# One pass for the normalised rows, and the first three tiles transposed before they are scaled: an attention and MLP kernel on one Trainium2 core

## The chip, the core and the metric

The kernel runs on one core of one Trainium2 chip. The core has a matrix engine (TensorE, "PE"; its weight loads are listed as "PEld"), three engines for everything else (VectorE "DVE", ScalarE "ACT", GpSimd "POOL") and a queue engine (SyncE, "SP") that here only issues DMA transfers. Each engine takes its instructions in the order of the program and waits on semaphores for the others. The metric is the device time of one execution in microseconds (us).

## The reference

`x` is a 2048 x 640 bfloat16 matrix. Each row is normalised, `xn = (x - m) / sqrt(v + eps)`. Two blocks read `xn`, and their results are added to `x`:

- a linear attention with 32 heads of 20: `q, k, v = xn @ wqkv`, `phi(t) = where(t > 0, t + 1, exp(t)) + 1e-6`, `kv = phi(k)^T v` and `z = sum of phi(k)` over all 2048 rows, then `o = phi(q) kv / (phi(q) z)` and `o @ wo`;
- a gated MLP on only 8 rows: `r = xn @ w_r` is computed for all rows, the 8 rows with the largest `r` go through `silu(x w_gate) * (x w_up) @ w_down`, are weighted with `sigmoid(r)` and added at their places.

## The kernel before, in words

The 2048 rows are 16 tiles of 128 rows. `XX` holds for each tile the rows as loaded (second index 1) and normalised (index 0); `xnT` holds the normalised rows transposed, which TensorE needs as its stationary operand. The order of the instructions is written out by hand in the program; there is no scheduler.

For a tile `t` these steps follow one another. `ln_a` and `ln_b` (VectorE, statistics of the two halves of the row, lines 161 and 164), `ln_g` (aggregate, 167), `ln_s` (add eps, line 200, then a power of one half on POOL, line 201): the row's standard deviation. For tiles 1 and 5 ScalarE makes the sums instead (`ln_act`, 175 to 179) and POOL the variance and the power (`ln_msq`, `ln_var`, 188 to 195). `ln_c` centres the row and flips its sign (on VectorE, line 208, or from tile 6 on ScalarE, line 206). `ln_xn` takes the reciprocal of the deviation (`SR`, line 213) and scales the centred row in a second VectorE pass (line 215). Tiles 0 to 3 are then transposed on TensorE into PSUM and copied to `xnT` by ScalarE (`tr_pe`, lines 222 and 226), the others by DMA transposes that SP issues (`tr_dma`, line 231).

`K(t)` multiplies the transposed tile with the key weights, in two halves of five matmuls (line 253); the second half carries `w_r` as a 321st column, so that `r` comes along. ScalarE applies exp and relu to each half (`PHe`, `PHr`, lines 269 and 272), VectorE joins them (`PHb`, line 288) to `pk`. `ones(t)` overwrites column 512 of the normalised tile with 1 (POOL, line 304), so that the product `G(t) = xn^T pk` (lines 293 and 298) also carries `z`; what belongs to that column is later restored in the value weights (`wv_rows`). K needs two PSUM banks that exp and relu of the tile before must have left.

Before the first tile, TensorE runs matmuls on zeros (`warm4`, fp32, line 122, and `warm`, bf16, line 127), with the small transpose of `w_r` between them.

The loop over tiles 4 to 15 keeps, at step t, K(t), PHb(t-1), the second pass and the DMA transpose of tile t+2, exp and relu of t, statistics and centring of t+3, statistics of t+4, and G(t-1). `loads(t)` issues later weights on SP. Behind the loop come the corner products (line 312), the query products (503), the kv and output-weight products, the MLP on the 8 rows, and the output (754, 768).

Of the kernel before, what the change touches and what calls it, by code (L numbers as in the profile page):

```python
# [27 lines left out]
TF = 11  # L28

# [9 lines left out]
def kernel(  # L39
# [39 lines left out]
    Gs = st([P, KC, D], BF16, "Gs")  # L79
# [10 lines left out]
    epsb = st([P, 1], BF16, "epsb")  # L90
# [12 lines left out]
    def ld(eng, dst, src):  # L103
        eng.dma_start(dst, src)
# [13 lines left out]
    zero32 = zero[:].bitcast(F32)  # L118

    def warm4(n):  # L120
        for _ in range(n):
            pe.matmul(PS[:, 7, :], lhsT=zero32[:, 0:P],
                      rhs=zero32[:, 0:256].unsqueeze(1).to_broadcast([P, 2, 256]), start=True, stop=True)
# [6 lines left out]
    pool.memset(epsb[:], EPS_BF16)  # L130
# [38 lines left out]
    cs = {}  # L169
# [15 lines left out]
    msq = st([P, 4], F32, "msq")  # L185

    def ln_msq(t):
        pool.tensor_tensor(out=msq[:, 0:1], in0=sm[:, t, 0:1], in1=sm[:, t, 0:1], op=ALU.mult)

    def ln_var(t):  # L190
        pool.tensor_tensor(out=MV[:, t, 1:2], in0=sm[:, t, 1:2], in1=msq[:, 0:1], op=ALU.subtract)
        t2 = tmp.tile([P, 1], BF16, tag="t2", name="t2", bufs=4)
        ss[t] = tmp.tile([P, 1], BF16, tag="s", name="s", bufs=4)
        pool.tensor_tensor(out=t2[:], in0=MV[:, t, 1:2], in1=epsb[:], op=ALU.add)
        pool.tensor_tensor(out=ss[t][:], in0=t2[:], in1=halfc[:], op=ALU.pow)

    def ln_s(t):
        t2 = tmp.tile([P, 1], BF16, tag="t2", name="t2", bufs=4)
        ss[t] = tmp.tile([P, 1], BF16, tag="s", name="s", bufs=4)
        dve.tensor_scalar(out=t2[:], in0=MV[:, t, 1:2], scalar1=EPS_BF16, scalar2=None, op0=ALU.add)  # L200
        pool.tensor_tensor(out=ss[t][:], in0=t2[:], in1=halfc[:], op=ALU.pow)  # L201

    def ln_c(t, eng):
        cs[t] = tmp.tile([P, D], BF16, tag="c", name="c", bufs=3)
        if eng is act:
            act.activation(cs[t][:], XX[:, t, 1, :], AF.Identity, bias=MVf[:, t, 0:1], scale=-1.0)  # L206
        else:
            dve.tensor_scalar(out=cs[t][:], in0=XX[:, t, 1, :], scalar1=MVf[:, t, 0:1], scalar2=-1.0,
                              op0=ALU.subtract, op1=ALU.mult)

    def ln_xn(t, parts=((0, D),)):
        c = cs[t]
        dve.reciprocal(SR[:, t : t + 1], ss[t][:])
        for a, b in parts:
            dve.tensor_scalar(out=XX[:, t, 0, a:b], in0=c[:, a:b], scalar1=SR[:, t : t + 1], scalar2=-1.0,  # L215
                              op0=ALU.mult, op1=ALU.mult)

    def tr_pe(t, b0, e0, e1, hs=(0, 1)):
        for b, k0, k1, eng in [((b0, 0, 3, e0), (b0 + 1, 3, KC, e1))[h] for h in hs]:
            pt = PS[:, b, :].bitcast(BF16)[:, 0 : (k1 - k0) * P]  # L220
            for kc in range(k0, k1):
                pe.transpose(pt[:, (kc - k0) * P : (kc - k0 + 1) * P], XX[:, t, 0, kc * P : (kc + 1) * P], ident[:])
            dst = xnT[:, k0:k1, t * P : (t + 1) * P]
            src = pt.rearrange("p (k c) -> p k c", c=P)
            if eng is act:
                act.copy(dst, src)  # L226
            else:
                dve.tensor_copy(dst, src)

# [19 lines left out]
    def K(t, hs=(0, 1), b=6):  # L249
        for h in hs:  # L250
            w = HW + h
            for kc in range(KC):
                pe.matmul(  # L253
                    PS[:, b + h, off(t, h) : off(t, h) + w],
                    lhsT=xnT[:, kc, t * P : (t + 1) * P],
                    rhs=wkh[h][:, kc, 0:w],
                    start=(kc == 0),
                    stop=(kc == KC - 1),
                )
# [5 lines left out]

    def PHe(t, h, b=6):
        if h == 0:
            phis[t] = tuple(tmp.tile([P, D], BF16, tag=k, name=k, bufs=3) for k in ("ek", "rk"))
        act.activation(phis[t][0][:, h * HW : (h + 1) * HW], phi_src(t, h, b), AF.Exp)  # L269

    def PHr(t, h, b=6):
        act.activation(phis[t][1][:, h * HW : (h + 1) * HW], phi_src(t, h, b), AF.Relu)  # L272
# [6 lines left out]
    def rcopy():  # L279
        act.copy(rbf[:, 0 : T - 2], PS[:, 7, HW : HW + T - 2])  # L280
        dve.tensor_copy(rbf[:, T - 1 : T], PS[:, 7, HW + T - 1 : HW + T])

    def rcopy1(b):
        act.copy(rbf[:, T - 2 : T - 1], PS[:, b, HW : HW + 1])
# [63 lines left out]
    pool_extra = {3: consts_b, 4: consts_c, 5: consts_d}  # L348
# [9 lines left out]
    def loads(t):  # L358
        if t < 5:
            ld(sp, XX[:, 6 + 2 * t : 8 + 2 * t, 1, :], x_v[:, 6 + 2 * t : 8 + 2 * t, :])  # L360
        if 7 <= t < 7 + KC:
            ld(sp, wv[:, t - 7, :], wqkv_v[:, t - 7, 2 * D : 3 * D])
        if t == 6:
            late["wvb"] = st([P, D], BF16, "wvb", "junk")
            ld(sp, late["wvb"][:], A_wqkv[ZD : ZD + 1, 2 * D : 3 * D].to_broadcast([P, D]))
# [20 lines left out]
    ln_msq(1)  # L386
    ln_c(0, dve)
    ln_c(1, dve)
    ln_xn(0, ((0, 3 * P), (3 * P, D)))
    tr_pe(0, 0, act, act)  # L390
    ln_var(1)
    ln_a(2)
    ln_xn(1)
    ln_b(2)
    ln_g(2)
    ln_s(2)
    ones(0)
    K(0, (0,))
    PHe(0, 0)
    tr_pe(1, 2, act, act)  # L400
    consts_e()
    bm2_copies(sp, (1, 2))
    PHr(0, 0)
    K(0, (1,))
    ln_c(2, dve)
    ln_a(3)
    ln_xn(2)
    PHa(0, (1,))
    K(1, (0,), 4)
    tr_pe(2, 0, act, act)  # L410
    K(1, (1,), 4)
    PHa(1, (0,), 4)
    PHa(1, (1,), 4)
    rcopy1(5)
# [116 lines left out]

    act.copy(Gs[:, 0, 0:512], PS[:, 0, :])
# [414 lines left out]
```

## Time and profile before

| | us |
|---|---|
| median of 3 runs | 109.26 (109.14 to 109.51) |
| profiled execution | 109.16 |
| its span, first to last instruction | 107.4 |
| TensorE busy | 101.6 |
| VectorE busy | 84.5 |
| ScalarE busy | 74.9 |
| POOL busy | 27.3 |

The span is 1.76 us shorter than the profiled execution's time; what lies around it is start and end. A view named "chain" follows the work that ended last back from the last instruction. In the views by line, a group's row gives the line, the engine, the operation, what it writes and reads, its shape and count, then the busy time of the group in us, the mean length of one in ns, and the idle time before them. In the timeline a row gives start and length in us; "x5" behind it means five instructions merged. Lengths overlap where an engine is pipelined: five matmuls of 0.3 us each can take 0.85 us together.

### The profile page before, as it was taken

The numbers are of one execution on the slowest core, as the hardware profiler recorded it, in microseconds if no ns is written. First come the engines' busy times: TensorE is split into PE (matmuls) and PEld (weight loads), VectorE is DVE, ScalarE is ACT, GpSimd is POOL, SyncE is SP. The second block draws the span as 40 slices with busy tenths as digits, with TensorE's granted clock in tenths as the row PEclk, the third lists the DMA queues.
The fourth block names the chain that finished last, engine by engine and source line by source line (L and its number), as shares of the span: only waits on it lengthen the run. The fifth ranks groups of instructions, "written<-read, shape, count | busy, mean of one in ns | idle before, by whom it ended". The sixth has DMA issues, their size and how long they took to land.

```text
span 107.4 us, 2577 instructions
## 1 busy us (share of the span) xinstructions
PE 101.6 (95%) x908; PEld 62.5 (58%) x918; DVE 84.5 (79%) x206; ACT 74.9 (70%) x163; POOL 27.3 (25%) x79
## 2 busy tenths in 40 slices
PE   5989999999999999999999999999999999999960
PEld 1245656666666666667556555655656677777740
DVE  1789997999989999974888987539599696888860
ACT  4649996888877777888596999988687699000000
POOL 7437235456222222000000683200008000000410
PEclk9999999999999999999999999999999999999999
DMA  2979971434555665889997999911650243895342
GB/s 70 296 215 324 324 143 38 84 76 77 131 127 122 128 127 120 183 233 367 265 402 259 313 338 383 309 43 36 205 179 0 62 146 111 213 368 191 126 132 65
DMA packets 23152, 19.68 MB, mean 183 GB/s; under 512 B 10595, under 2 KB 21603, under 8 KB 23139
## 3 DMA queue, kind: packets, MB, share of 16 engines
q1 hardware_dynamic: 21944, 19.00, 60.7%
q10 hardware_dynamic: 906, 0.50, 1.6%
q8 instruction: 7, 0.11, 0.4%
q0 software_dynamic: 288, 0.01, 0.3%
q14 instruction: 7, 0.05, 0.2%
HBM read 13.80 MB, written 3.65 MB: 162 GB/s over the span
## 4 chain that ended last, share of the span: by engine, by line
PE 82%; DVE 7%; DMA 2%; POOL 2%; issue 2%; ACT 1%; SPq 0%; POOLq 0%
PE PS L503 20%; PE PS L754 20%; PE PS L253 15%; PE PS L293 14%; PE PS L298 4%; DMA XX<-in_A_x_dram 2%; PE PS L679 2%; PE PS L716 2%; DVE XX L215 1%; DVE pk L288 1%; POOL s L201 1%; DVE stats L164 1%; PE PS L567 1%; PE PS L738 1%; PE PS L312 1%
## 5 line engine op out<-in xcount | busy, mean ns | idle before, releaser
L253 PE MATMUL PS<-wk,xnT 128*128 128x320 bf16 (+1 forms) x160 | 24.7, 300 | 0.4 <-ACT xnT L226 0.4
L503 PE MATMUL PS<-xnT,wq 128*128 128x512 bf16 x95 | 22.7, 380 | 0.3
L293 PE MATMUL PS<-pk,XX 128*128 128x512 bf16 x75 | 22.3, 379 | 0.2 <-DVE pk L288 0.2
L754 PE MATMUL PS<-Mb,pqT 128*128 128x320 bf16 x160 | 22.1, 299 | 0.0
L253 PEld LDWEIGHTS <-xnT 128*128 128x128 bf16 x160 | 15.4, 98 | 7.3 <-ACT xnT L226 0.9
L754 PEld LDWEIGHTS <-pqT 128*128 128x128 bf16 x160 | 15.5, 97 | 6.5 <-issue 0.2
L269 ACT ACTIVATE ek<-PS 128x320 bf16<-128x320 f32 x32 | 14.2, 445 | 5.2 <-PE PS L253 5.2
L503 PEld LDWEIGHTS <-wq 128*128 128x128 bf16 x100 | 11.3, 118 | 9.0
L558 DVE SCALAR_TENSOR_TENSOR pqT<-qe,qr 128x512 bf16<-128x512 bf16 x20 | 13.5, 684 | 2.0 <-ACT qr L510 1.7
L768 DVE TENSOR_TENSOR o<-PS,XX 128x640 bf16<-128x640 f32 x15 | 12.2, 821 | 3.5 <-PE PS L754 2.8
L509 ACT ACTIVATE qe<-PS 128x512 bf16<-128x512 f32 x20 | 12.2, 609 | 3.8 <-PE PS L503 3.3
L272 ACT ACTIVATE rk<-PS 128x320 bf16<-128x320 f32 x32 | 14.3, 447 | 0.0
L298 PE MATMUL PS<-pk,XX 128*128 128x128 bf16 x64 | 14.0, 219 | 0.3
L201 POOL TENSOR_TENSOR s<-t,halfc 128x1 bf16<-128x1 bf16 x14 | 8.7, 625 | 21.6 <-DVE t L200 21.6
L288 DVE SCALAR_TENSOR_TENSOR pk<-ek,rk 128x640 bf16<-128x640 bf16 x16 | 13.0, 815 | 0.9 <-ACT rk L272 0.7
L293 PEld LDWEIGHTS <-XX 128*128 128x128 bf16 x80 | 7.7, 98 | 8.1
L510 ACT ACTIVATE qr<-PS 128x512 bf16<-128x512 f32 x20 | 12.1, 605 | 0.0
L206 ACT ACTIVATE c<-XX,MVf 128x640 bf16<-128x640 bf16 x10 | 8.4, 839 | 1.7 <-DVE MVf L167 1.6
L243 ACT ACTIVATE XX<-XX,MR,SR 128x640 bf16<-128x640 bf16 x11 | 9.4, 915 | 0.0
L161 DVE BATCH_NORM_STATS2 stats<-XX 128x6 f32<-128x320 bf16 x14 | 6.8, 485 | 1.9 <-DMA XX<-in_A_x_dram 1.9
L215 DVE TENSOR_SCALAR XX<-c,SR 128x640 bf16<-128x640 bf16 (+2 forms) x17 | 6.3, 377 | 1.3
L593 DVE TENSOR_TENSOR pqT<-pqT,R 128x1280 bf16<-128x1280 bf16 x8 | 6.5, 817 | 0.5 <-DMA R<-rd_d 0.5
(125 smaller groups left out, 104.7 us busy)
## 6 DMA issues: line engine op xcount, KB each, us to landing
out_dram<-o SPq DMA_DIRECT2D x15, 160.0 KB, 2.8
XX<-in_A_x_dram SPq DMA_DIRECT2D x6, 320.0 KB, 5.2
wg<-in_B_w_gate_dram SPq DMA_DIRECT2D x5, 384.0 KB, 8.1
wu<-in_B_w_up_dram SPq DMA_DIRECT2D x5, 384.0 KB, 5.9
wd<-in_B_w_down_dram SPq DMA_DIRECT2D x1, 1920.0 KB, 11.3
wv<-in_A_wqkv_dram SPq DMA_DIRECT2D x5, 160.0 KB, 3.0
wq<-in_A_wqkv_dram SPq DMA_DIRECT2D x1, 800.0 KB, 5.0
hi_d<-XX SPq DMA_DIRECT2D x1, 800.0 KB, 4.5
```

What stands on the lines that cost most here:

```text
L253: pe.matmul(PS[:, b + h, off(t, h) : off(t, h) + w], lhsT=xnT[:, kc, t * P : (t + 1) * P], rhs=wkh[h][:, kc, 0:w], start=(kc == 0), stop=( ...
L269: act.activation(phis[t][0][:, h * HW : (h + 1) * HW], phi_src(t, h, b), AF.Exp)
L272: act.activation(phis[t][1][:, h * HW : (h + 1) * HW], phi_src(t, h, b), AF.Relu)
L288: dve.scalar_tensor_tensor(out=pk[:, t, :], in0=ek[:], scalar=1.0, in1=rk[:], op0=ALU.min, op1=ALU.add)
L293: pe.matmul(PS[:, a, :], lhsT=lhsT, rhs=pk[:, t, 0:512], start=(t == 0), stop=(t == T - 1),)
L298: pe.matmul(PS[:, 5, a * P : (a + 1) * P], lhsT=lhsT, rhs=pk[:, t, 512:D], start=(t == 0 and a == 0), stop=(t == T - 1), skip_group_check= ...
L503: pe.matmul(PS[:, bank, :], lhsT=by5(wq[:, kc, :])[:, m, :], rhs=xnT[:, kc, tb * TBLK : (tb + 1) * TBLK], start=(kc == 0), stop=(kc == KC ...
L509: act.activation(e, PS[:, bank, :], AF.Exp)
L510: act.activation(r, PS[:, bank, :], AF.Relu)
L558: dve.scalar_tensor_tensor(out=pqT[:, m, tb * TBLK : (tb + 1) * TBLK], in0=e, scalar=1.0, in1=r, op0=ALU.min, op1=ALU.add,)
L754: pe.matmul(PS[:, b + h, 0:HW], lhsT=pqT[:, kc, t * P : (t + 1) * P], rhs=Mb[:, kc, h * HW : (h + 1) * HW], start=(kc == 0), stop=(kc == K ...
L768: dve.tensor_tensor(out=ot[:].rearrange("p (h c) -> p h c", h=2), in0=PS[:, b : b + 2, 0:HW], in1=XX[:, t, 1, :].rearrange("p (h c) -> p h ...
```

## The change

- `ln_n` makes the normalised row in one VectorE pass, `(x - mean) * SR`, with both scalars taken per row from memory; `ln_xn` is reciprocal plus that pass. The centring passes `ln_c` of tiles 3 and later are gone (ten of them were on ScalarE).
- Tiles 0 to 2 (`CT = 3`) are only centred (`ln_c`, without the flipped sign) and transposed on TensorE in that state into a new tile `cT`. Their K uses `cT`; exp and relu multiply by the row's factor `SR` (`scale=SR`), and the two copies of `r` of tiles 0 and 1 do too. `cT` shares its memory with `Gs`, which is now allocated after the loop.
- Their normalised rows are made later (`ln_n(0)`, `ln_n(1)`, `ln_n(2)`), for G alone, and their transposes for `xnT` are three DMA transposes, at t = 5, 7 and 9. As column 512 has been overwritten by then, POOL first keeps it (`keep512`), and three small DMAs on ScalarE's queue put it back into `xnT` at t = 12 (`back512`).
- Of the PSUM copies of `tr_pe`, tile 0's first half and tile 2's second half go to VectorE.
- The warm-up is one fp32 matmul on a constant that is there earlier, and behind the transpose of `w_r` 20 matmuls of 96 columns, in place of a second fp32 one and one of 512 columns.
- POOL's variance takes one instruction less (`ln_msqe` folds eps in). `consts_e` moves from the start to the loop (after G(6)); the three copies of `bm2` move to ScalarE's queue at t = 10; the loads of `wv` and `wvb` move from SP's queue to ScalarE's.
- The order of the first tiles is rewritten.

```diff
+    def warm4():
+        pe.matmul(PS[:, 7, 0:512], lhsT=z0.to_broadcast([P, P]), rhs=z0.to_broadcast([P, 512]), start=True, stop=True)
...
-    warm4(1)
+    warm4()
     pe.transpose(PS[:, 3, :].bitcast(BF16)[:, 0:KC], wr[:], ident[0:KC, 0:KC])
-    warm4(1)
-    warm(1)
+    warm(20, 96)
...
+    def ln_msqe(t):
+        pool.tensor_scalar(out=msqe[:, t : t + 1], in0=sm[:, t, 0:1], scalar1=sm[:, t, 0:1], scalar2=EPS_BF16,
+                           op0=ALU.mult, op1=ALU.subtract)
...
+    def ln_r(t):
+        dve.reciprocal(SR[:, t : t + 1], ss[t][:])
+
+    def ln_n(t, parts=((0, D),), eng=dve):
+        for a, b in parts:
+            eng.tensor_scalar(out=XX[:, t, 0, a:b], in0=XX[:, t, 1, a:b], scalar1=MVf[:, t, 0:1],
+                              scalar2=SR[:, t : t + 1], op0=ALU.subtract, op1=ALU.mult)
...
+    def ln_c(t):
+        cs[t] = tmp.tile([P, D], BF16, tag="c", name="c", bufs=CT)
+        dve.tensor_scalar(out=cs[t][:], in0=XX[:, t, 1, :], scalar1=MVf[:, t, 0:1], scalar2=None, op0=ALU.subtract)
+
+    def keep512(t):
+        pool.tensor_copy(c512[:, t : t + 1], XX[:, t, 0, ZD : ZD + 1])
+
+    def back512():
+        for t in range(CT):
+            ld(act, xnT[0:1, KC - 1, t * P : (t + 1) * P], c512[:, t : t + 1])
...
-                    lhsT=xnT[:, kc, t * P : (t + 1) * P],
+                    lhsT=(cT if t < CT else xnT)[:, kc, t * P : (t + 1) * P],
...
+    def row_scale(t):
+        return {"scale": SR[:, t : t + 1]} if t < CT else {}
...
-        act.activation(phis[t][0][:, h * HW : (h + 1) * HW], phi_src(t, h, b), AF.Exp)
+        act.activation(phis[t][0][:, h * HW : (h + 1) * HW], phi_src(t, h, b), AF.Exp, **row_scale(t))
...
+    ln_c(0)
+    ln_c(1)
+    tr_pe(0, 0, dve, act, 3)
+    tr_pe(1, 2, act, act)
     ln_var(1)
+    ln_r(0)
+    K(0, (0,))
     ln_a(2)
     ln_b(2)
     ln_g(2)
+    ln_c(2)
     ln_s(2)
+    ln_r(1)
+    PHa(0, (0,))
+    K(1, (0,), 4)
     ln_a(3)
     ln_b(3)
     ln_g(3)
     ln_s(3)
+    PHa(1, (0,), 4)
+    tr_pe(2, 0, act, dve)
+    K(0, (1,))
+    ln_r(2)
+    ln_n(0)
+    keep512(0)
+    ones(0)
+    PHa(0, (1,))
+    K(1, (1,), 4)
+    PHa(1, (1,), 4)
+    rcopy1(5)
+    ln_xn(3)
     PHb(0)
+    K(2)
+    PHa(2, (0,))
+    tr_pe(3, 2, act, act)
+    PHa(2, (1,))
     ln_a(4)
     ln_b(4)
     ln_g(4)
     ln_s(4)
+    PHb(1)
     ln_xn(4)
     tr_dma(4)
+    ln_n(1)
+    keep512(1)
+    ones(1)
     ln_act(5)
+    ln_msqe(5)
     G(0, (0, 1, 4, 2, 3))
     K(3)
     G(1)
+    ln_n(2)
+    keep512(2)
+    ones(2)
     PHb(2)
     ln_var(5)
     PHa(3)
+    ln_a(6)
     ln_xn(5)
     tr_dma(5)
+    ln_b(6)
     ln_g(6)
     ln_s(6)
     ones(3)
     G(2)
...
-            ln_c(t + 3, act)
...
+        if t in (5, 7, 9):
+            tr_dma((t - 5) // 2)
         if t > 4:
             loads(t)
+        if t == 10:
+            bm2_copies(act, (1, 2, 3))
+        if t == 12:
+            back512()
```

More of the change, by code (lines that the diff above doesn't have):

```diff
@@ L28 @@
 TF = 11
+CT = 3
 BF16 = mybir.dt.bfloat16
@@ L115 @@
     ld(sp, XX[:, 2, 1, :], x_v[:, 2, :])
[L118 to L123, printed above, removed]
+    z0 = nc.const_aps.tensor(0.0, [P, 1], F32)
+    def warm4():
+        pe.matmul(PS[:, 7, 0:512], lhsT=z0.to_broadcast([P, P]), rhs=z0.to_broadcast([P, 512]), start=True, stop=True)
     def warm(n, w=512):
@@ L190, in ln_var @@
     def ln_var(t):
-        pool.tensor_tensor(out=MV[:, t, 1:2], in0=sm[:, t, 1:2], in1=msq[:, 0:1], op=ALU.subtract)
         t2 = tmp.tile([P, 1], BF16, tag="t2", name="t2", bufs=4)
-        ss[t] = tmp.tile([P, 1], BF16, tag="s", name="s", bufs=4)
-        pool.tensor_tensor(out=t2[:], in0=MV[:, t, 1:2], in1=epsb[:], op=ALU.add)
-        pool.tensor_tensor(out=ss[t][:], in0=t2[:], in1=halfc[:], op=ALU.pow)
+        pool.tensor_tensor(out=t2[:], in0=sm[:, t, 1:2], in1=msqe[:, t : t + 1], op=ALU.subtract)
@@ L197, in ln_s @@
+        ln_pow(t, t2)
     def ln_s(t):
         t2 = tmp.tile([P, 1], BF16, tag="t2", name="t2", bufs=4)
-        ss[t] = tmp.tile([P, 1], BF16, tag="s", name="s", bufs=4)
         dve.tensor_scalar(out=t2[:], in0=MV[:, t, 1:2], scalar1=EPS_BF16, scalar2=None, op0=ALU.add)
[L201 to L209, printed above, removed]
@@ L211, in ln_xn @@
-    def ln_xn(t, parts=((0, D),)):
[L212 to L219, printed above, removed]
+        ln_pow(t, t2)
+    def ln_r(t):
+        dve.reciprocal(SR[:, t : t + 1], ss[t][:])
@@ L221, in tr_pe @@
             for kc in range(k0, k1):
[L222 to L223 removed]
+                src = cs[t][:, kc * P : (kc + 1) * P] if t < CT else XX[:, t, 0, kc * P : (kc + 1) * P]
+                pe.transpose(pt[:, (kc - k0) * P : (kc - k0 + 1) * P], src, ident[:])
+            dst = (cT if t < CT else xnT)[:, k0:k1, t * P : (t + 1) * P]
             src = pt.rearrange("p (k c) -> p k c", c=P)
```

74 lines of the change are left out of this document (20 added, 54 removed).

## The prediction

> **What bounds the kernel now.** I read the page first (span, busy time, chain shares), then busy time by stretches, then the chain in order of time, and last the instructions one by one up to 24 us.
>
> ```profile
> span 107.4 us, 2577 instructions
> ...
> PE 101.6 (95%) x908; PEld 62.5 (58%) x918; DVE 84.5 (79%) x206; ACT 74.9 (70%) x163; POOL 27.3 (25%) x79
> ...
> PE 82%; DVE 7%; DMA 2%; POOL 2%; issue 2%; ACT 1%; SPq 0%; POOLq 0%
> ```
>
> PE carries 82% of the chain. Where it doesn't is seen in the stretches (columns: PE, PEld, DVE, ACT, POOL busy, clock, DMA) and the chain:
>
> ```profile
> 14.00:16.00 2.00, 1.85 (x14) 1.08 (x12) 1.97 (x5) 1.97 (x7) 0.42 (x2) 1.00 0.64 83
> 16.00:18.00 2.00, 2.00 (x15) 1.12 (x14) 1.34 (x6) 1.12 (x5) 1.05 (x3) 1.00 0.31 63
> ```
>
> ```profile
> 9.58 0.41 DVE stats L164
> ...
> 10.71 0.73 DVE pk L288
> ...
> 13.25 0.62 POOL s L201
> ...
> 14.49 0.74 DVE pk L288
> ...
> 15.28 0.38 PE PS L293
> ...
> 18.04 1.37 PE PS L253 x10
> ...
> 22.09 0.27 PE PS L293
> ...
> 50.19 0.84 PE PS L312 x15
> ```
>
> Up to 15.28 the chain runs through VectorE and the short POOL powers; from there it is matmuls without a hole, K(4) at 18.04, G(4) at 22.09, the corners at 50.19. (The chain puts a matmul some 0.16 later than its start, since the one before ends then: K(4) starts at 17.88, G(4) at 21.93.) So all that the change can win lies ahead of about 22 us. Behind it PE has the same work, and each 0.1 us by which G(4) is early is 0.1 us of the end, unless a later wait takes it back.
>
> **The start.** PE and VectorE rows of the first 12 us:
>
> ```profile
> 3.35 2.08 PE L122 MATMUL PS<-zero 128*128 128x512 f32 x2
> 5.22 0.63 PE L127 MATMUL PS<-zero 128*128 128x512 bf16 x1
> 5.90 0.71 PE L222 MATMUL PS<-ident,XX 128*128 128x128 bf16 x5
> 6.97 0.85 PE L253 MATMUL PS<-wk,xnT 128*128 128x320 bf16 x5 [0.36 <-ACT xnT L226]
> 7.66 0.44 PE L222 MATMUL PS<-ident,XX 128*128 128x128 bf16 x5
> ```
>
> ```profile
> L222 PE MATMUL PS<-ident,XX x20: 219/219/314, 5.9 to 12.2; 128*128 128x128 bf16 x20
> ```
>
> ```profile
> 4.37 0.88 DVE L208 TENSOR_SCALAR c<-XX,MVf 128x640 bf16<-128x640 bf16 x2
> ```
>
> ```profile
> 8.18 0.38 DVE L208 TENSOR_SCALAR c<-XX,MVf 128x640 bf16<-128x640 bf16 x1
> ```
>
> Tile 0's transposes now wait for power, reciprocal and second pass until 5.90; centred rows exist at 4.75 (two passes of 0.38 from 4.37, the second waits for ScalarE's mean and ends at 5.25). Five transposes took 0.71 with 0.314 for the last, so 0.10 each at 5.90, and (0.44-0.219)/4 = 0.055 each at 7.66: the array ran at half speed until past 6.3, at full speed from 6.97, where K took (0.85-0.30)/4 = 0.137 a matmul. The clock column shows 1.00 throughout, so only these steps tell it.
>
> After the change the second fp32 block and the 512-wide warm-up (until 5.65) become 20 matmuls of 96 columns from 3.42. At half speed the 96 columns cost 96/128 of 0.105, i.e. 0.08: they end at 5.0. The bound above is the full 0.10 to 0.107 of a 128-column pair, if the weight load paces them (end 5.5); below, 0.04 at full speed, but then c0 at 4.8 is the limit. I take 0.08. Transposes of tiles 0 and 1 follow back to back (10 x 0.105) to 6.0, and K(0) starts at 6.0 for 6.97. VectorE copies tile 0's first half from 5.5 (third transpose plus 0.31).
>
> **VectorE's queue.** Prices, and steps: an instruction that doesn't read the one ahead starts 0.08 before that ends (statistics 0.485 long, 0.41 apart above).
>
> ```profile
> L288 DVE SCALAR_TENSOR_TENSOR pk<-ek,rk 128x640 bf16<-128x640 bf16 x16 | 13.0, 815 | 0.9 <-ACT rk L272 0.7
> ...
> L161 DVE BATCH_NORM_STATS2 stats<-XX 128x6 f32<-128x320 bf16 x14 | 6.8, 485 | 1.9 <-DMA XX<-in_A_x_dram 1.9
> ...
> L215 DVE TENSOR_SCALAR XX<-c,SR 128x640 bf16<-128x640 bf16 x15 | 5.8, 387 | 1.3
> ...
> L167 DVE BATCH_NORM_AGGREGATE MVf<-stats 128x2 bf16<-128x12 f32 x14 | 3.0, 211 | 0.5
> ...
> L208 DVE TENSOR_SCALAR c<-XX,MVf 128x640 bf16<-128x640 bf16 x6 | 2.3, 379 | 0.1
> ...
> L240 DVE TENSOR_SCALAR XX<-XX,SR,MR 128x640 bf16<-128x640 bf16 x5 | 2.0, 443 | 0.0
> ...
> L733 DVE COPY hT<-PS 128x384 bf16<-128x384 bf16 x1 | 0.4, 358 | 0.0
> ```
>
> The one-pass row takes two per-partition scalars, like L240: 0.443, 0.06 over L215's 0.387 (the bounds). Up to tile 5 VectorE loses three centring passes (c of 3, 4, 5: 3 x 0.30), gains two PSUM copies (0.29 and some 0.23) and 6 x 0.06: even. What it gains is idle time and an earlier start. Adding the steps in the new order: copy 5.5, reciprocal 5.8, tile 2's statistics 5.87, c(2) 7.05 (for 8.18), tile 3's statistics 7.48, n(0) 9.0, n(3) 9.75, PHb(0) 10.1 (for 10.71), G(0) 11.05. Tile 4's statistics 10.85, PHb(1) 12.1 (for 14.49: two n-passes now stand behind it), n(4) 13.1, n(1) 13.5-13.9, so G(1) 13.97 for 15.28 and K(4) 16.57 for 17.88: **1.3 us ahead**. The transposes by DMA keep up:
>
> ```profile
> xnT<-XX SPq DMA_TRANSPOSE x12, 2.6
> ```
>
> n(4) ends at 13.55, plus 2.6 is 16.2.
>
> **What is late next.** POOL, then VectorE again:
>
> ```profile
> 14.92 0.36 POOL L188 TENSOR_TENSOR msq<-sm 128x1 f32<-128x1 f32 x1 [1.00 <-ACT junk L175]
> 15.94 0.37 POOL L191 TENSOR_TENSOR MVf<-sm,msq 128x1 bf16<-128x1 f32 x1 [0.66 <-ACT junk L179]
> 16.38 0.19 POOL L194 TENSOR_TENSOR t<-MVf,epsb 128x1 bf16<-128x1 bf16 x1
> 16.66 0.55 POOL L195 TENSOR_TENSOR s<-t,halfc 128x1 bf16<-128x1 bf16 x1
> ```
>
> ```profile
> L304 POOL MEMSET XX<- 128x1 bf16 x16 | 1.5, 100 | 3.7 <-DMA xnT<-XX 3.7
> ```
>
> ```profile
> 17.24 0.16 DVE L213 RECIPROCAL SR<-s 128x1 f32<-128x1 bf16 x1 [0.58 <-POOL s L195]
> ...
> 18.05 0.82 DVE L288 SCALAR_TENSOR_TENSOR pk<-ek,rk 128x640 bf16<-128x640 bf16 x1
> ...
> 21.12 0.81 DVE L288 SCALAR_TENSOR_TENSOR pk<-ek,rk 128x640 bf16<-128x640 bf16 x1
> ```
>
> Tile 5's power now stands on POOL behind keep512 and ones of tiles 1 and 2: from n(1)'s end at 13.9, copy, memset, msq, copy, memset, subtract, power. A 128x1 copy isn't in the trace; the nearest rows are 0.19 and 0.37, I take 0.28, so 0.28+0.1+0.36+0.28+0.1+0.28+0.55 plus gaps of 0.08 (16.57 to 16.66) = 2.2, and reciprocal(5) starts at 16.2 (for 17.24; at 0.19 and 0.37 each it is 15.85 and 16.5). Then n(5) 16.4, aggregate(6) 17.3, PHb(3) 17.6 to 18.45 (for 18.05). PE reaches G(3) at 16.57+1.37 = 17.94 and waits 0.56. PHb(4), seven steps on with the dearer n(6), comes at 20.57 to 21.4 (for 21.12 to 21.93), K(5) ends at 21.17, another 0.28 lost. G(4) at 21.45 for 21.99 (PHb(4)'s end and 0.06): **0.55 us ahead**. From there VectorE's steps add up to 2.55 a tile (PHb 0.735, two statistics 0.81, n 0.36, aggregate, reciprocal and the small ones 0.65) for PE's 2.68 (from 18.04 to 22.09 less one K of 1.37), and nothing holds PE.
>
> **ScalarE and the queues.** Ten centring passes go, DMA issues come:
>
> ```profile
> 12.55 0.60 ACTq L104 DMA_DIRECT2D bm<-bm  x1
> ```
>
> ```profile
> L206 ACT ACTIVATE c<-XX,MVf 128x640 bf16<-128x640 bf16 x10 | 8.4, 839 | 1.7 <-DVE MVf L167 1.6
> ```
>
> One issue a tile (0.6) for 0.84 of work is no loss. At t = 10 there are four (wv and three bm2, 2.4), at t = 12 three (1.8). ScalarE has 1.2 free between relu(t) and K(t+1)'s first half; the issue of 12.55 ran under two queued copies, so some 0.5 more is covered, and exp(11) is 0.7 late, exp(13) 0.1. Behind them wait PHb(11) and K(12), which has G(10)'s 1.3 as slack. Taken at nothing; with no cover the four cost 0.5. The transposes' issue on SP:
>
> ```profile
> 27.59 1.22 SPq L231 DMA_TRANSPOSE xnT<-XX  x1
> ```
>
> bm2 leaves SP's queue ahead of tr_dma(4), which waits for n(4) anyway; the extra transposes at t = 5, 7, 9 take 1.2 of SP each, where 2.67 is there for two and the loads have gone to ScalarE's queue. back512 lands 8 us before the first query product at 51. Scaled exp and relu: between the same and 0.08 more (L240 over L215, as for VectorE); hidden, as VectorE is behind.
>
> **The sum.** Profiled run 109.16 (span 107.4 and 1.76 around it) minus 0.55 is 108.6; the median of three, 109.26, is 0.1 above the profiled run, so I say **108.7**. About 0.3%, 0.33 us, is what a measurement here can tell from no change.
>
> **Rivals.** (1) *Slower: the full clock comes a stretch later.* The speed-up seen between 6.3 and 6.97 followed dense fp32 and 512-wide matmuls; now short matmuls and ten transposes stand there. PE is nearly back to back from 6.0 to 10.65 in my sum (30 K matmuls of 0.137). If it stays at half speed until about 10, some 3.5 us later, G(0) comes 1.7 later, of which VectorE's lag covers 0.4: 108.7+1.3 = 110.0. It takes back all 0.55 from a grant at about 8.5 on (half of 1.9 us, less the 0.4). Against it: PE is fed without a gap from 3.42, no less than before. The Trainium skill ("TensorE: Matmul & The Clock Gate", Part 4) says that transposes on TensorE don't count as busy for the clock gate; by that, what counts between 3.4 and 6.0 is 1.6 us of warm-ups where it was 2.5, and this rival would come. The trace has transposes at full speed at 7.66, but no speed-up after transposes alone, so it leaves the rule open. Chance 0.20.
>
> (2) *No change: the warm-ups are paced by their weight loads* (0.105) or the POOL copies take 0.37: each takes back 0.3 to 0.5 of the 0.55, since both stand in series with VectorE's queue: 109.1 to 109.2. For it: transposes step at 0.10 to 0.107, POOL rows beside busy VectorE are at 0.36. The four issues at t = 10 uncovered end here too. Chance 0.20.
>
> (3) *More: POOL's short ops at 0.19 and passes at 0.387*: 0.3 each, 108.1. Chance 0.15. My own case 0.45, by itself 108.4 to 109.0.
>
> **Range and chances.** 107.9 (both gains of 3) to 109.8 (most of rival 1). Faster by over 0.3%: three quarters of mine, all of (3), a quarter of (2): 0.54. Slower: 0.19 of (1) and 0.04 elsewhere: 0.23. The rest, 0.23, is the same.
>
> **What would show it.** Warm-ups 0.08 apart, K(0) near 6.0 in steps of 0.27 then 0.137, n(3) near 9.75, G(1) near 14.0, reciprocal(5) idle on POOL until 16.2, PE idle ahead of G(3) and G(4) and nowhere after, corners near 49.6 in the chain's count, passes of 0.44. Wrong if K still steps at 0.27 past 8, or if PE has holes after 30 us.

## The result, and the profile after

The changed kernel takes 113.63 us (median of 4 executions, 112.87 to 114.62) where the kernel before takes 109.2 us. The profiled execution (114.62 us, span 112.9 us) holds a stretch of half clock between 50 and 53 us, worth 1.6 us there, so its ratio is taken from the other three: their median is 113.40 us, 1.038 times as long, with a 95% interval of 1.032 to 1.044. The forecast was 108.7 us and faster.

The page of the kernel after: span, busy time, the chain by engine, and the group of the K matmuls.

```profile
span 112.9 us, 2604 instructions
...
PE 104.1 (92%) x935; PEld 64.0 (57%) x935; DVE 85.0 (75%) x204; ACT 68.0 (60%) x151; POOL 28.3 (25%) x79
...
PE 57%; DVE 15%; DMA 13%; POOL 5%; ACT 3%; issue 2%; ACTq 1%; SPq 1%; DVEq 0%
...
L262 PE MATMUL PS<-wk,xnT 128*128 128x320 bf16 (+1 forms) x130 | 20.4, 304 | 3.8 <-DMA xnT<-XX 3.7
```

TensorE carried 82% of the chain before and carries 57% now; DMA went from 2% to 13%. The idle time ahead of K names the cause's place: 3.7 us of waiting for transposes by DMA. TensorE's timeline of the kernel after shows where (start, length, then in brackets the idle time ahead and what ended it):

```profile
4.76 1.04 PE L216 MATMUL PS<-ident,c 128*128 128x128 bf16 x10
5.71 0.45 PE L262 MATMUL PS<-wk,cT 128*128 128x320 bf16 x2
6.81 1.25 PE L262 MATMUL PS<-wk,cT 128*128 128x320 bf16 x8 [0.65 <-DMA wk<-in_A_wqkv_dram]
...
18.68 1.54 PE L262 MATMUL PS<-wk,xnT 128*128 128x320 bf16 x10 [0.95 <-DMA xnT<-XX]
...
23.02 0.38 PE L306 MATMUL PS<-pk,XX 128*128 128x512 bf16 x1
...
30.26 1.55 PE L262 MATMUL PS<-wk,xnT 128*128 128x320 bf16 x10 [0.42 <-DMA xnT<-XX]
...
48.83 1.95 PE L262 MATMUL PS<-wk,xnT 128*128 128x320 bf16 x10 [2.35 <-DMA xnT<-XX]
...
53.13 1.58 PE L262 MATMUL PS<-wk,xnT 128*128 128x320 bf16 x10
```

The rows of the same work in the kernel before, G(4), K(8), K(14) and K(15):

```profile
21.98 0.38 PE L293 MATMUL PS<-pk,XX 128*128 128x512 bf16 x1
...
28.63 1.54 PE L253 MATMUL PS<-wk,xnT 128*128 128x320 bf16 x10
...
44.68 1.54 PE L253 MATMUL PS<-wk,xnT 128*128 128x320 bf16 x10
...
47.35 0.84 PE L253 MATMUL PS<-wk,xnT 128*128 128x320 bf16 x5
```

So the kernel after is 1.04 us late at G(4), 1.63 at K(8), 4.15 at K(14) and 5.78 at K(15). The steps are 1.0 at the start, 0.6 at K(8), 2.5 ahead of K(14), and 1.6 of half clock in this execution alone. The chain of the kernel after gives the transposes behind two of them, and three rows of the start:

```profile
12.58 1.07 POOL s L187
...
14.74 1.09 POOL c L233
...
17.37 0.17 DVE SR L200
...
25.91 4.30 DMA xnT<-XX
...
42.49 6.29 DMA xnT<-XX
```

A transpose by DMA had taken 2.6 us from issue to landing; that of tile 8 takes 4.30 and that of tile 14 takes 6.29. The stretches around it (columns as in the prediction; the last two are the share of the DMA engines and GB/s), after and then before:

```profile
44.00:46.00 2.00, 2.00 (x16) 1.25 (x15) 1.93 (x7) 1.26 (x4) 0.16 (x2) 1.00 1.26 121
46.00:48.00 2.00, 0.48 (x3) 0.10 (x1) 1.83 (x5) 0.96 (x2) 0.00 (x0) 1.00 1.08 75
48.00:50.00 2.00, 1.17 (x8) 0.82 (x9) 0.13 (x1) 0.22 (x1) 0.10 (x1) 0.95 1.60 82
50.00:52.00 2.00, 2.00 (x8) 0.96 (x7) 0.39 (x1) 1.73 (x5) 0.07 (x1) 0.50 0.60 159
```

```profile
44.00:46.00 2.00, 2.00 (x16) 1.29 (x15) 1.88 (x5) 1.55 (x5) 0.00 (x0) 1.00 0.91 168
46.00:48.00 2.00, 2.00 (x16) 1.21 (x15) 1.26 (x3) 1.84 (x5) 0.10 (x1) 1.00 0.83 235
```

From 46 to 48 us the share of the DMA engines rises from 0.83 before to 1.08 after, while they move a third of the bytes (75 GB/s for 235): something occupies them without moving much data. (A packet is counted in the stretch in which it starts, so a share can exceed 1.) Transfers issued in that stretch land late, whatever they carry; the rows of the issues (KB each, then us to landing) from 40 to 56 us:

```profile
wq<-in_A_wqkv_dram SPq DMA_DIRECT2D x1, 800.0 KB, 7.9
wo<-in_A_wo_dram SPq DMA_DIRECT2D x4, 160.0 KB, 7.0
...
xnT<-XX SPq DMA_TRANSPOSE x3, 6.3
xnT<-c ACTq DMA_DIRECT2D x3, 0.2 KB, 6.9
```

Before, wq took 5.0 us there and the four wo transfers 2.9.

### The profile page after: what moved, and what is told of

It reads as the page before. It is cut to its first block, busy times and chain, and to the rows that moved or that the text cites. A ratio compares the mean times of both kernels' runs of the same rounds, so it can differ in the third digit from the quotient of the medians.

```text
span 112.9 us, 2604 instructions
## 1 busy us (share of the span) xinstructions
PE 104.1 (92%) x935; PEld 64.0 (57%) x935; DVE 85.0 (75%) x204; ACT 68.0 (60%) x151; POOL 28.3 (25%) x79
## 4 chain that ended last, share of the span: by engine, by line
PE 57%; DVE 15%; DMA 13%; POOL 5%; ACT 3%; issue 2%; ACTq 1%; SPq 1%; DVEq 0%
PE PS L517 20%; PE PS L769 19%; DMA xnT<-XX 9%; PE PS L262 5%; PE PS L306 5%; DMA XX<-in_A_x_dram 4%; DVE pk L301 3%; POOL s L187 3%; DVE XX L204 3%; DVE stats L159 3%; DVE stats L156 2%; ACT rk L284 2%; PE PS L694 1%; PE PS L731 1%; DVE MVf L162 1%
## 5 line engine op out<-in xcount | busy, mean ns | idle before, releaser
L306 PE MATMUL PS<-pk,XX 128*128 128x512 bf16 x80 | 24.8, 395 | 0.3 <-ACT xnT L220 0.3
L262 PE MATMUL PS<-wk,xnT 128*128 128x320 bf16 (+1 forms) x130 | 20.4, 304 | 3.8 <-DMA xnT<-XX 3.7
L281 ACT ACTIVATE ek<-PS 128x320 bf16<-128x320 f32 x26 | 11.4, 437 | 19.8 <-PE PS L262 16.7
L262 PEld LDWEIGHTS <-xnT 128*128 128x128 bf16 x130 | 12.5, 99 | 10.5 <-DMA xnT<-XX 5.2
L187 POOL TENSOR_TENSOR s<-t,halfc 128x1 bf16<-128x1 bf16 x16 | 10.1, 632 | 22.8 <-DVE t L196 21.3
L306 PEld LDWEIGHTS <-XX 128*128 128x128 bf16 x80 | 7.9, 101 | 9.3 <-issue 1.1
L524 ACT ACTIVATE qr<-PS 128x512 bf16<-128x512 f32 x20 | 12.1, 607 | 0.0
L284 ACT ACTIVATE rk<-PS 128x320 bf16<-128x320 f32 x26 | 11.3, 435 | 0.0
L204 DVE TENSOR_SCALAR XX<-XX,MVf,SR 128x640 bf16<-128x640 bf16 x16 | 7.0, 445 | 0.5
L311 PEld LDWEIGHTS <-XX 128*128 128x128 bf16 x64 | 6.4, 101 | 1.4 <-issue 0.6
```

The source lines that it names most:

```text
L262: pe.matmul(PS[:, b + h, off(t, h) : off(t, h) + w], lhsT=(cT if t < CT else xnT)[:, kc, t * P : (t + 1) * P], rhs=wkh[h][:, kc, 0:w], sta ...
L306: pe.matmul(PS[:, a, :], lhsT=lhsT, rhs=pk[:, t, 0:512], start=(t == 0), stop=(t == T - 1),)
L311: pe.matmul(PS[:, 5, a * P : (a + 1) * P], lhsT=lhsT, rhs=pk[:, t, 512:D], start=(t == 0 and a == 0), stop=(t == T - 1), skip_group_check= ...
L524: act.activation(r, PS[:, bank, :], AF.Relu)
```

## The experiments

**What makes the hole ahead of K(14)?** Theory A: the three transfers of back512 hold up the others. B: the additional transposes on SP's queue. C: the loads moved to ScalarE's queue. The first four runs take one away each.

```diff
         if t == 12:
-            back512()
```

> The changed kernel without back512, the three transfers of 128 two-byte elements each that write the kept columns into xnT; the first row of the last block of xnT then holds ones for tiles 0 to 2, so this part of the result is left wrong. Theory A (these three transfers occupy the DMA engines that the transposes of tiles 14 and 15 and the load of wq need): the transpose of tile 14, issued near 42.5 us, lands some 2.6 to 3 us later instead of 6.3, the hole of TensorE ahead of K(14) near 46 to 49 us (2.35 us) closes, the time falls by 2.2 to 2.8 us to 110.6 to 111.4 us, and what is left over the kernel before is K(4), K(5) and K(8). Theory B (the additional transposes of tiles 0 to 2 on SP's queue push the regular ones back): the hole stays, 113 us. Theory C (the loads moved to ScalarE's queue share the DMA engines with the transposes): the hole stays, 113 us.

Measured: 110.72 us, 1.010 times the kernel before (1.003 to 1.017). There is no wait ahead of K(14); tile 14's transpose, issued at 42.0 us, lands 2.6 us later. A holds, by 2.7 us (113.40 to 110.72). K(4), K(5), K(8) and K(11) still wait, 0.30 to 0.48 us each.

```diff
-        if t in (5, 7, 9):
-            tr_dma((t - 5) // 2)
```

> The changed kernel without the later transposes by DMA of tiles 0 to 2; POOL sets that part of xnT to zero instead, so the query side of tiles 0 to 2 is left out of the result; back512 stays. Theory A: the hole ahead of K(14) stays at 2 us or more; only K(8)'s wait (0.67 us) can go, so 112.5 to 113.6 us. Theory B: the waits ahead of K(8) and K(14) both go, 110 to 110.5 us. Theory C: as A, but with K(8)'s wait kept: 113 to 113.6 us.

Measured: 114.18 us, 1.043 times (1.035 to 1.050): no gain at all. B falls. The two rows of TensorE's timeline that decide it, K(8) and K(14):

```profile
30.20 1.55 PE L262 MATMUL PS<-wk,xnT 128*128 128x320 bf16 x10 [0.42 <-DMA xnT<-XX]
...
48.78 1.55 PE L262 MATMUL PS<-wk,xnT 128*128 128x320 bf16 x10 [2.36 <-DMA xnT<-XX]
```

```diff
-            ld(act, wv[:, t - 7, :], ...)
+            ld(sp, wv[:, t - 7, :], ...)
-            ld(act, late["wvb"][:], ...)
+            ld(sp, late["wvb"][:], ...)
```

> The changed kernel with the loads of wv and wvb issued from SP again, behind the transposes, as before the change. Theory A: K(8)'s wait (0.67 us) goes if the broadcast load of wvb on ScalarE's queue was what delayed the transpose of tile 8 (landing 4.3 us after its issue; it should be 2.6), the hole ahead of K(14) stays: 112.5 to 113.2 us. Theory C: both go: 110 to 110.6 us. Theory B: SP's queue becomes longer still (0.6 us for each load), both stay or grow: 113.4 us or more.

Measured: 112.14 to 115.66 us, median 113.76: 112.14 and 112.41 at a granted clock of 1.0, 115.10 and 115.66 at a mean of 0.985. K(8) no longer waits, since tile 8's transpose now lands 3.0 us after its issue in place of 4.3, but the hole ahead of K(14) stays (2.15 us). C is right for K(8) and wrong for K(14). A fetch of instructions, told of below, also falls at another place of that flight here (1.1 us after the issue, 2.5 there), so the wvb load and the fetch are not told apart for K(8)'s 0.6 us.

```diff
     def back512():
+        row = PS[:, 6, :].bitcast(BF16)[0:1, 2 * HW : 2 * HW + CT * P]
         for t in range(CT):
-            ld(act, xnT[0:1, KC - 1, t * P : (t + 1) * P], c512[:, t : t + 1])
+            pe.transpose(row[:, t * P : (t + 1) * P], c512[:, t : t + 1], ident[:])
+        dve.tensor_copy(xnT[0:1, KC - 1, 0 : CT * P], row)
```

> The changed kernel with back512 done on chip without DMA: three TensorE transposes of a 128x1 column each into the free end of bank 6 and one VectorE copy of 384 elements into the row of xnT. Theory A: as without back512, plus three transposes (0.1 us each) on TensorE and one copy (some 0.3 to 0.5 us) on VectorE: 110.8 to 111.8 us. Theories B and C: 113.4 us or more.

Measured: 111.95 us, a little above what was expected. The hole is gone, but K(14) waits 0.49 us for VectorE's copy out of the bank it needs.

**Is it the transfers by themselves, and what about them?** Theory A left two readings: 384 elements of two bytes, or all of them into one partition. Both runs add transfers to the kernel *before*, and differ only in the destination.

```diff
+        if t == 12:
+            for k in range(3):
+                ld(act, Gs[0:1, 0, k * P : (k + 1) * P], XX[:, k, 0, ZD : ZD + 1])
```

> The kernel before, with only the three transfers of back512 added: column 512 of tiles 0 to 2 is written by ScalarE's queue, at the same place of the loop, into one row of Gs, which nothing reads before it is overwritten. Theory A (three transfers of 128 two-byte elements into one partition hold up the other transfers): the transpose of tile 15 (issued 43.3, landed 46.1 us in the kernel before, used at 47.35 us) or the load of wq (landed 49.5, used at 50.9 us) comes late by 2 to 4 us, TensorE gets a hole of 1 to 3 us between 44 and 54 us, and the time is 110.5 to 112.5 us. If the transfers are harmless and the hole comes from what else the change does: 109.2 to 109.6 us.

```diff
-                ld(act, Gs[0:1, 0, k * P : (k + 1) * P], XX[:, k, 0, ZD : ZD + 1])
+                ld(act, Gs[:, 0, k : k + 1], XX[:, k, 0, ZD : ZD + 1])
```

> As the run with the transfers in the kernel before, but each writes its 128 two-byte elements down a column of Gs, one into each of 128 partitions, in place of along a row of one partition; number and size of the elements are the same. Theory A1 (what costs is that all elements go to one partition): 109.2 to 109.6 us, no new hole. Theory A2 (what costs is the number of two-byte elements): the same loss as with the row, 110.5 to 112.5 us.

Measured: along a row, 111.47 us at a granted clock of 0.999, and 113.2 to 114.2 in three executions at a mean of 0.984 to 0.985; down a column, 109.11 us, 0.9996 times (0.998 to 1.002). The same stretch of both, the row first; and the row's wait ahead of K(15):

```profile
46.00:48.00 2.00, 1.70 (x12) 0.81 (x10) 1.84 (x5) 2.00 (x6) 0.00 (x0) 1.00 1.72 55
```

```profile
46.00:48.00 2.00, 2.00 (x16) 1.22 (x15) 1.83 (x5) 2.00 (x5) 0.10 (x1) 1.00 0.83 248
```

```profile
49.91 2.70 PE L253 MATMUL PS<-wk,xnT 128*128 128x320 bf16 x10 [2.21 <-DMA xnT<-XX]
```

Three small transfers are enough for such a hole, in a kernel that has nothing else of the change, and it is the destination that decides: with the elements spread over 128 partitions the engines move 248 GB/s in the stretch where they move 55 with all of them in one. The row also puts the 128 elements side by side into 256 bytes; no run tells the single partition from this adjacency. The Trainium skill ("DMA: Bandwidth & Descriptors", Specifications) says that transfers below 512 bytes are done by reading, modifying and writing; by that rule both forms should cost alike, and they don't: at this size and number the measurement finds no cost in the small elements as such.

```diff
-            for k in range(3):
-                ld(act, Gs[0:1, 0, k * P : (k + 1) * P], XX[:, k, 0, ZD : ZD + 1])
+            for k in range(6):
+                ld(act, Gs[0:1, k // 5, k % 5 * P : (k % 5 + 1) * P], XX[:, k, 0, ZD : ZD + 1])
```

> The kernel before with six transfers of 128 two-byte elements into one partition in place of three. If the elements are written one after another into the partition and hold up what comes behind them, the stretch with little traffic of DMA ahead of K(15) grows with their number: with three the transpose of tile 15 came some 3.5 us late (hole 2.2 us, slack 1.3 us), so with six 6 to 8 us late, a hole of 5 to 7 us, 115 to 118 us. If the cost is one for each time that such transfers meet the others, not for each element, the hole stays near 2.2 us: 111.5 to 113.5 us.

Measured: 115.15 us, 1.054 times (1.048 to 1.060), at the low edge of the first expectation. Tile 15's transpose, issued at 43.3 us, lands 8.9 us later; with three it had taken 6.4 and with none 2.8. So the delay grows by 1.2 us for each of the first three transfers of 128 elements and by 0.8 for each of the next three. The time is not that of the transfers alone: all four executions ran at a mean granted clock of 0.97 to 0.985. The hole itself comes another way: five of the issues on ScalarE's queue took 5.61 us, the exp that stands behind them waits, and K(14) is held by ScalarE.

```profile
42.04 5.61 ACTq L104 DMA_DIRECT2D Gs<-XX  x5
47.75 0.44 ACT L269 ACTIVATE ek<-PS 128x320 bf16<-128x320 f32 x1 [5.42 <-DMA wo<-in_A_wo_dram]
```

**What is left without back512?** About 1.4 us. The next runs compute the whole result without it: POOL copies the column back into the tile, the transpose by DMA carries it, and POOL sets the ones again; wv is on SP's queue.

```diff
+    def put512(t):
+        pool.tensor_copy(XX[:, t, 0, ZD : ZD + 1], c512[:, t : t + 1])
...
         ones(t)
+        if t in (4, 6, 8):
+            put512((t - 4) // 2)
+        if t in (7, 9, 11):
+            ones((t - 7) // 2)
```

> The changed kernel without back512 and with wv and wvb loaded from SP's queue again: POOL copies the kept column back into the tile before its transpose by DMA and sets it to one again two tiles later, so that the transpose itself brings the row into xnT, and the whole result is computed. Theory A with the wvb load as the cause of K(8)'s wait: no hole ahead of K(14) and none over 0.3 us ahead of K(8); K(5)'s wait (0.3 to 0.5 us) stays; 109.3 to 110.2 us. If the additional transposes are a cost of their own (they take SP 1.2 us each): 110.5 us or more.

Measured: 110.79 us, 1.016 times (1.008 to 1.023): K(8) and K(14) don't wait, but K(4) (0.36), K(5) (0.55) and K(12) (0.31) do. Of these 1.22 us, 0.91 stand ahead of K(4) and K(5), before the first additional transpose is issued (24.67 us); at most K(12)'s 0.31 can be the work of those transposes.

```diff
-    for t in range(1, 5):
+    for t in range(1, 3):
         loads(t)
...
     tr_dma(4)
+    loads(3)
+    loads(4)
```

> As the run before it, and the loads of x for tiles 12 to 15 are issued behind the transpose of tile 4 in place of ahead of it. If the transpose of tile 4 lands late (4.3 us after its issue in the changed kernel) because it stands behind the loads of x: it lands within 3 us, K(4) starts near 17.0 to 17.5 us, and the time is 0.3 to 1 us below the run before it, 108.5 to 109.5 us. If it is late for another reason, K(4) starts where it did and the two agree.

Measured: 111.29 us, 1.015 times (1.009 to 1.020), no better. K(4) starts at 17.74 us, but the loads now stand ahead of tile 5's transpose, which lands 4.45 us after its issue, and K(5) waits 1.44 us. The wait moved by one tile.

The next two take POOL's copies out of the start: `keep512` is gone, and `put512` works the column out as centred value times `SR` (first diff, both runs). One of them, e12, also issues the transpose of zeros ahead of most loads of x, and the last load in the loop (second diff).

```diff
-        pool.tensor_copy(XX[:, t, 0, ZD : ZD + 1], c512[:, t : t + 1])
+        pool.tensor_scalar(out=XX[:, t, 0, ZD : ZD + 1], in0=cs[t][:, ZD : ZD + 1], scalar1=SR[:, t : t + 1],
+                           scalar2=None, op0=ALU.mult)
```

```diff
     loads(0)
-    for t in range(1, 5):
+    sp.dma_start_transpose(xnT[:, 0:4, S - P : S], zero[:])
+    for t in range(1, 4):
         loads(t)
-    sp.dma_start_transpose(xnT[:, 0:4, S - P : S], zero[:])
...
+        if t == 5:
+            loads(4)
```

> The changed kernel without back512, wv and wvb on SP's queue, and three more edits: the columns are not kept at the start (POOL works column 512 out again from the centred row, before the transpose by DMA), the transpose of zeros is issued ahead of most loads of x, and the load of x for tiles 14 and 15 is issued in the loop at tile 5. If the late transposes of tiles 4 and 5 are what is left of the loss: K(4) near 17.2 to 17.5 us, K(5) near 20 to 20.3 us without a wait, and 108.4 to 109.2 us. If something else delays the transposes: 110 us or more.

> As the run before it, but with the order of SP's queue left as in the changed kernel. If POOL's copies (1.08 us for the one beside a VectorE pass) set when tile 5 is normalised: its reciprocal near 16.3 in place of 17.4 us, its transpose issued near 16.9 us, K(5) without a wait but K(4) still late (17.8 to 18.5 us): 109.3 to 110 us. If not, 110.4 to 110.9 us.

Measured: 110.89 us, 1.014 times (1.009 to 1.019), and 110.45 us, 1.011 times (1.005 to 1.018). The reciprocal of tile 5 starts at 16.47 us in e13, 0.9 us sooner than in the changed kernel, so POOL's copies did set it; K(4) is on time there (17.20 us, wait 0.12). K(5) still waits 0.55 us (the expectation had it on time): its transpose, issued sooner, lands 3.56 us after its issue, and K(12) waits 0.93. In e12 K(4) and K(5) still wait 0.41 and 0.43 us, and K(10) waits 1.41 us for a transpose of 4.88 us.

**Is one part of the change harmless?** The rows in one pass, alone, in the kernel before, from tile 3 on:

```diff
+        if t > 2:
+            dve.tensor_scalar(out=XX[:, t, 0, :], in0=XX[:, t, 1, :], scalar1=MVf[:, t, 0:1],
+                              scalar2=SR[:, t : t + 1], op0=ALU.subtract, op1=ALU.mult)
+            return
...
-    ln_c(3, dve)
```

(and so for the other centring passes of tiles 3 and later)

> The kernel before with one part of the change alone: from tile 3 on the normalised rows come from one VectorE pass over x (mean subtracted, then times the row factor) in place of a centred copy and a second pass; tiles 0 to 2, their transposes, the warm-ups and the DMA queues stay as before. If TensorE is bound by its own work from 8 us on, as its idle time between 8 and 54 us in the kernel before says (under 0.4 us), this part moves the time by no more than that: 108.9 to 109.3 us. If the passes are on the path at the start (tiles 3 to 5), up to 0.5 us faster: 108.6 to 108.9 us.

Measured: 110.73 us, 1.011 times (1.006 to 1.015): slower, which neither expectation had. The traced execution (111.43 us) is the slowest of six, which took 110.16 to 110.41 and 111.05 to 111.43. K(4) starts at 19.16 us in it, 1.28 later than in the kernel before, and this lateness stands ahead of the first row in one pass (12.51 us). Three rows of its chain:

```profile
1.25 3.10 DMA XX<-in_A_x_dram
...
5.46 0.39 DVE c L208
...
7.40 1.52 PE PS L256 x5
```

ScalarE waited for the load of x of tile 1, TensorE idled for 0.48 us ahead of the first transposes, and K(0)'s five matmuls took 1.52 us where they had taken 0.85: full speed, as read from such steps, came later. The edit touches nothing that runs so early, and the other executions differ by nearly as much, so this is taken for a difference of the start, not for the price of the rows. Behind it the kernel has one more wait, ahead of K(5):

```profile
22.85 1.55 PE L256 MATMUL PS<-wk,xnT 128*128 128x320 bf16 x10 [0.86 <-DMA xnT<-XX]
```

No load is under way during that transpose. What stands beside it, in this run and in every one above that has the one-pass rows, is a packet of 8 KB on a queue that the page calls instruction: the fetch of a block of instructions. VectorE has begun 50 instructions when it comes in nine of the kernels with such rows (52 in e7) and 65 in four with two passes, so the fetch was taken for VectorE's. With the five memsets of the test below the counts are 53, 54 and 63 and not 50 and 65, so whose fetch it is stays open. Theory F: a fetch in the flight of a transpose delays its landing. The test adds short instructions to VectorE to move the fetch.

```diff
-    dve.memset(eps6[:], 1e-6)
+    for _ in range(6):
+        dve.memset(eps6[:], 1e-6)
```

> As the run with POOL's copies removed and the order of SP's queue left (110.45 us), with five more VectorE memsets of one element a partition in the idle time at the start. Theory F (the fetch of 8 KB belongs to VectorE's instructions and delays a transpose in whose flight it falls): the fetch that came at 19.2 us comes near 17.6 us, the transpose of tile 5 lands 2.6 us after its issue in place of 3.6, K(5) starts without a wait (0.55 us there), and the time falls by about 0.5 us to 109.7 to 110.1 us. Rival (the late landing comes from the transposes and loads in flight): the landing stays near 3.5 us and the time at 110.3 to 110.7 us.

> The kernel before with one-pass rows alone (110.73 us) and five more VectorE memsets of one element a partition in the idle time at the start. Theory F: the fetch that came at 21.2 us comes near 19.4 us, the transpose of tile 5 lands within 2.6 us, K(5)'s wait (0.86 us) goes, and the time is 109.2 to 109.9 us. Rival: K(5)'s wait stays, 110.3 to 110.9 us.

> The kernel before with the five memsets alone. They stand in VectorE's idle time ahead of the first load of x, so that by themselves they cost nothing; the fetch at 23.28 us moves to 21 to 22 us, where the transpose of tile 6 (issued 20.0 us) may be in flight, which has 0.7 us to spare ahead of K(6). Theory F: 109.1 to 109.6 us, with the transpose of tile 6 landing 3 to 3.5 us after its issue if the fetch comes 1 to 2 us after it. Rival: 109.1 to 109.4 us with 2.6 us.

The rows of single transposes follow (us to landing last; a row of the instruction queue gives packets, MB and share of the DMA engines). The kernel before, tile 5; then without POOL's copies (fetch 2.0 us after the issue) and with the memsets (1.1 us after):

```profile
xnT<-XX SPq DMA_TRANSPOSE x1, 2.6
```

```profile
q14 instruction: 1, 0.01, 0.8%
...
xnT<-XX SPq DMA_TRANSPOSE x1, 3.6
```

```profile
q14 instruction: 1, 0.01, 1.1%
...
xnT<-XX SPq DMA_TRANSPOSE x1, 3.1
```

And the kernel before with the memsets, tile 6, where the fetch has moved from 23.28 to 21.29 us, 1.2 us after that transpose's issue (without them it lands in 2.6 us):

```profile
q14 instruction: 1, 0.01, 1.0%
...
xnT<-XX SPq DMA_TRANSPOSE x1, 3.0
```

The one-pass kernel goes from 3.4 to 3.0 us in the same way, and its wait ahead of K(5) from 0.86 to 0.13. The memsets moved the fetch by less than expected, so it didn't leave the flight; but where it falls sooner in the flight the landing is sooner, and in the control, where it is moved *into* a flight, a landing that had been on time is late. Theory F holds for the landing, each from one traced execution. In e14 to e17 the fetch comes 1.1 to 1.2 us after the issue, and the landing takes 3.0 to 3.1 us; at tile 5 of e10, of the changed kernel and of e1 to e4, e9 and e13 it comes 1.8 to 2.0 us after, and the landing takes 3.4 to 3.6. Tile 7 of e5 and e11, at which no run was aimed, fits (1.1 us after; 2.97 and 2.98 us), beside 2.62 and 2.63 in the kernel before and e8, where the fetch comes 0.7 to 0.8 us after the issue.

For the time it isn't shown. One pass with memsets takes 110.01 us, 1.0036 times (1.001 to 1.006), against 110.73 without, but its traced execution starts K(4) 0.71 us sooner, a difference of the start as told above, and of the 0.73 us by which K(5)'s wait shrinks the landing gives 0.42. The faster three executions without memsets (110.16 to 110.41) are 0.15 to 0.4 us above 110.01. The chain of the run with memsets shows what is left of it:

```profile
10.78 1.06 POOL s L202
11.87 0.17 DVE SR L213
```

Tile 3's power on POOL takes 1.06 us there, beside PHb(0), which starts sooner (10.61 us) now that tile 3's centring pass is gone; the reciprocal waits 0.44 us for it, and K(4) starts 0.57 us later than in the kernel before.

The control takes 109.35 us (0.997 to 1.003 times), since K(6) has the time to spare. In e14 the time doesn't fall: 110.76 us, 1.010 times (1.006 to 1.014). K(5) is on time, and K(12) waits longer:

```profile
17.93 1.55 PE L259 MATMUL PS<-wk,xnT 128*128 128x320 bf16 x10 [0.31 <-DMA xnT<-XX]
...
41.30 1.55 PE L259 MATMUL PS<-wk,xnT 128*128 128x320 bf16 x10 [1.32 <-DMA xnT<-XX]
```

Last, the additional transposes ahead of the loads of wv:

```diff
-        if t in (5, 7, 9):
-            tr_dma((t - 5) // 2)
+        if t in (4, 5, 6):
+            tr_dma(t - 4)
```

(`put512` and the later `ones` move with them.)

> As the run before it, with the later transposes of tiles 0 to 2 issued at tiles 4, 5 and 6 of the loop, ahead of the loads of wv and wvb, in place of tiles 5, 7 and 9 among them. If K(12)'s wait (0.9 us in the run with POOL's copies removed, its transpose landing 4.0 us after its issue) comes from transposes and loads of wv in flight together: that wait goes, and the time is 108.7 to 109.3 us. If not: 109.7 to 110.3 us.

Measured: 110.58 us, 1.010 times (1.006 to 1.013). K(12)'s wait goes and K(9) gets one of 0.92 us, for a transpose of 3.67 us. No arrangement tried here comes below the kernel before. An estimate by subtraction shows no sign of a gain either: e14 without its two waits (0.31 and 1.32) would have a span of 107.6 us, beside 107.4.

## Why the prediction was wrong, step by step

- **The start: right.** Warm-ups 0.08 apart, K(0) at 5.71 us (forecast 6.0), the pass at 0.445 us (0.443), n(3) at 9.84 us (9.75). Two K matmuls in 0.45 us leave a step of 0.15, so the full clock was there by 5.7 us, sooner than before, and rival 1 fell. The rule of the Trainium skill ("TensorE: Matmul & The Clock Gate", Part 4) that it was weighed with stays open: the clock rose during the ten transposes, behind 1.8 us of warm-ups, which may have been enough. Not foreseen: the wait for the rest of wk at 6.81 us.
- **VectorE and POOL up to G(1): right in kind, short in size.** G(1) came at 14.73 us, 0.54 sooner than before and not 1.3. Of the 0.76 that is missing, 0.31 stands at PHb(1) (12.41 us for 12.1): the wait for wk, and ScalarE, which runs without a gap from 7.41 to 10.40 us with its scaled passes at 0.57 us on average for 0.44, the price that the sum had called hidden. The other 0.45 is the wait of tile 4's reciprocal for POOL: its power took 1.07 us (0.62 in the kernel before) beside PHb(1), a VectorE pass with two operands. The kept column took 1.09 where the bound was 0.37; it starts 0.21 us ahead of PHb(2) and ends just behind it, so which pass held it isn't told apart. The two other copies took 0.19. The trace of before had such a row, a power that starts beside PHb(3) (18.05 us), and the sum passed it by:

```profile
18.22 1.06 POOL L201 TENSOR_TENSOR s<-t,halfc 128x1 bf16<-128x1 bf16 x1 [1.01 <-DVE t L200]
```

  The Trainium skill ("SBUF — State Buffer", SBUF: two separate sides) says that a VectorE pass with two operands in memory and a POOL instruction that reads memory hold a port in turn, each for its whole length; for the power the traces agree (1.06 to 1.07 us beside such a pass, 0.55 to 0.74 otherwise).
- **"The transposes by DMA keep up": wrong.** The step added the median landing of 2.6 us to n(4)'s end. At K(4) the landing took 4.3 us (issue at 14.35), at K(5) 3.5, at K(8) 4.3. The median came from the kernel before, where eight of ten such transposes land in 2.56 to 2.62 us, among loads too; in the changed kernel other transfers fall into these flights: a fetch at K(5), the wvb load and a fetch at K(8), several at K(4). With this, the forecast of 0.55 us ahead at G(4) became 1.04 behind.
- **"back512 lands 8 us before the first query product at 51": the step that failed.** Only its landing was priced; what it does to transfers in flight beside it was put at nothing. It did land in time, 5.5 us ahead of that product, but the three row-wise transfers held tile 14's transpose for 6.29 us (2.6 without them) and TensorE for 2.35. That cost 2.7 us (e1), the largest term of the 4.2; e5 alone adds such a hole, and e8, down a column, doesn't.
- **The rivals.** None of them was the one that came. "PE has holes after 30 us" was named as what would prove the forecast wrong, but no transfer was named as its cause; rival 1 had the right sign by another mechanism.
- **Open.** K(4)'s lateness varies between runs (a wait of 0.1 to 0.95 us); loads of x, the transpose of zeros and a 16 KB fetch meet there, and no run separates them. The start varies between executions (e10), and one trace for each run can't take that out of the small differences. It was not traced why transposes among loads of 160 KB land in 3.4 to 4.9 us at one place and 2.6 at another.

## What to carry to other kernels

Price a transfer by what else is in flight when it runs, not only by when its reader needs it: one that writes many two-byte elements along a row of one partition delayed a transpose beside it by 0.8 to 1.2 us per 128 elements here, while the same elements into 128 partitions cost nothing that could be measured. When work is moved onto a path of transposes with half a microsecond of slack, a median landing time is no cover; list the slack of each. And an edit that only changes how many instructions an engine has can move a fetch of instructions into such a flight: when a small change costs more than its instructions, look at the instruction queue in the trace. Compare the starts of two traced executions before a difference of some tenths of a microsecond is put to an edit.

## What the runs showed of the hardware that was not expected

- Transfers of 128 two-byte elements along a row of one partition: the DMA share goes to 1.72 at 55 GB/s with three of them (0.83 at 248 GB/s when the destination is a column), and the transpose behind them lands 2.8, 6.4 and 8.9 us after its issue with none, three and six.
- A transpose by DMA of the kernel before lands in 2.56 to 2.62 us in eight of ten flights; with an 8 KB fetch of instructions 1.1 us after its issue in 3.0 to 3.1 us, 1.8 to 2.0 us after it in 3.4 to 3.6.
- A hole of TensorE of over 2 us was followed in some executions by half clock: 0.50 in the stretch from 50 to 52 us of the changed kernel, while the run without the additional transposes kept 1.00 behind a hole of 2.36 us.
